# Agent attention with a routed feed-forward on one core: the folded units' matrix in one pass, its low part on spare rows

## The chip, the cores and the metric

The kernel runs on one core of a Trainium2 chip. The metric is the device time of one execution in microseconds (us). Three timed runs of the kernel before gave 667.96, 669.16 and 669.85 us; their median is 669.16 us. A fourth execution was profiled: it took 664.34 us, of which 662.6 us lie between the first and the last instruction, and all rows below are of this one.

## The reference

Four batches of 11,456 tokens with 128 channels go through an attention over 49 agents, and then through a layer of eight experts of which each token takes one.

```
def sm(a, b):
    s = scale * (a @ b.transpose(0, 2, 1))
    s = s - s.max(-1, keepdims=True)
    e = np.exp(s)
    return e / (e.sum(-1, keepdims=True) + 1e-09)
a2k = sm(agents, k)
agent_v = a2k @ v
q2a = sm(q, agents)
x = q2a @ agent_v
...
expert_idx = np.argmax(logits, axis=1)          # logits: cosine of x and each expert's row, over tau
for e in range(E):
    mask = expert_idx == e
    h = np.maximum(x[mask] @ w1[e], 0.0)
    out[mask] = gate_w[mask, None] * (h @ w2[e])
```

Here E is 8, w1 is 128 by 1024 and w2 is 1024 by 128 for each expert.

## The kernel before, in words

**A token is 49 exponentials.** Its x is a mix of 49 agent rows. The kernel never forms x: it keeps the token's 49 exponentials e, multiplies the agent rows into the expert's first matrix once a batch (one row g of 49 numbers for each of the 1024 hidden units), and computes a hidden unit as relu(g . e). The division by the sum of e, and the gate, come at the end as one factor per token.

**Three kinds of units.** All e are positive, so a unit whose g has mostly one sign keeps its sign over nearly all tokens. `pick_expert(b, g)` takes one expert for the whole batch, gives each unit a key for how much its sign is in doubt, and ranks the units by it. The `FM` = 256 units in most doubt are computed in full as a layer (`gh`, `gl`, the high and low float16 parts of their g, and `w2p`, their rows of w2). The others are taken as always on or always off: those that are on are summed into one 49 by 128 matrix, `lin`, so that their share of the output is e times `lin`. The next `FV` = 288 units in rank are checked for every token, by a product with `vm` (their g, times their sign, less a safety margin): the first `NEAR` = 32 with a minimum for each token (`vmin`), the other 256 with a sum of negative parts for each pair of tokens (`vsum`). For the units beyond, one bound on the token (`far`) does. Tokens that fail, or whose expert is another one, are done again at the end in full (`mark_strays`, `fix`, `stray`): 128 places a batch in `fix`, one group in `stray_first`, and what is then left in a loop at the end of the program (L1740), of one pass for each 128 places.

**Operands.** `q_unit` makes the exponentials of a unit of 8 columns of 128 tokens: 128 partitions (tokens) by 8 columns by 128 places, of which places 0 to 48 hold the high float16 part, 64 to 112 the low part, and the 30 others zero. A transposing DMA on the queue of SP (SyncE) turns each column, so that `tt` has the 128 places on partitions. There are 48 such units, 12 a batch.

**Tiles.** The feed-forward goes over 92 tiles (23 a batch) of four columns, 512 tokens (the last of a batch has two columns of 96). `ffn_mm1` (L1237, L1238) does a half of 128 layer units by two matmuls of 512 columns; ScalarE takes the relu into a high part (L1246), VectorE the low part (L1247). `ffn_mm2` adds into the tile's `yp`, at f = 0, the folded part: for each column two matmuls of 128 columns, one with the high and one with the low part of `lin` (L1261). Then each of the two halves gives three matmuls a column (L1273 to L1275; L1270 for tiles from 16 on of the first three batches). VectorE multiplies by the gate into `ot` (L1289), and ScalarE's queue stores it.

```
1258:            for c in range(n):
1259:                tc_ = tts[b, u][:, (w * TJ + c) * p : (w * TJ + c + 1) * p]
1260:                for h in range(2):
1261:                    pe.matmul(out=yp[:p, c, :], lhsT=tc_, rhs=bt.lin[:, h], start=(c == 0 and h == 0), stop=False, skip_group_check=True)
```

**The check.** `proved` does a unit's check in five jobs: 8 matmuls of 32 columns and VectorE's minimum (L1092, L1095), and four pairs of matmuls of 256 columns with ScalarE's sum (L1089, L1098).

**Order.** Beside the feed-forward of a batch the kernel loads the keys, values and queries of the next one by a plan of due times, makes its scores and its exponentials, and near the batch's end runs `pick_expert` for the next. SP's queue stands in an order written out; on the other engines a scheduler that runs a model of the program sets the order, so that an edit in one place moves instructions elsewhere too.

Of the kernel before, what the change touches and what calls it, by code (L numbers as in the profile page):

```python
# [29 lines left out]
def kernel(ctx: ExitStack, tc: tile.TileContext, q, k, v, agents, emb, tau, w1, w2, out):  # L30
# [8 lines left out]
    NEAR = 32  # L39
    FV = 2 * P + NEAR  # L40
    FM = NM * P
    FW = 4 * P
# [13 lines left out]
    LO = 64  # L56
# [243 lines left out]
    tri = cst.tile([P, P], F16, name="tri")  # L300
    uid = cst.tile([P, NF], I32, name="uid")
# [22 lines left out]
    def setup():  # L324
# [4 lines left out]
        with tc.issue_after(turned[0].ins):  # L329
# [7 lines left out]
            dve.tensor_tensor(out=fold, in0=ident[:, :A], in1=ident[:, LO : LO + A], op=ALU.add)  # L337
            pool.iota(tok[:, :, :J], pattern=[[N, B], [1, J]], base=0, channel_multiplier=J,
# [236 lines left out]
    def av_chain(b, g):  # L575
# [45 lines left out]
        dve.tensor_copy(r_hi[:, E : E + 1], ones[:, :1])  # L621
# [48 lines left out]
    def pick_expert(b, g):  # L670
# [173 lines left out]
        gmx = sm.tile([P, 2], F32, name="gmx", tag="gmx")  # L844
        yield 2 * g
        act.copy(gh, placed(0, FM))
        yield g
        dve.tensor_copy(gl, placed(1, FM))
        bt.gh, bt.gl = gh, gl
        dve.tensor_reduce(out=gmx[:, :1], in_=ga, axis=AX.XY, op=ALU.max, apply_absolute_value=True)  # L850
# [4 lines left out]
        dve.tensor_scalar(mask, rank, FM + FV - 0.5, BIG, ALU.is_lt, ALU.mult)  # L855
# [3 lines left out]
        dve.tensor_reduce(out=gmx[:, 1:], in_=mask, axis=AX.X, op=ALU.min)  # L859
        yield 1  # L860
        dve.tensor_scalar(gmx[:, 1:], gmx[:, 1:], -1.0, None, ALU.mult)
        dve.tensor_scalar(mask, rank, FM - 0.5, None, ALU.is_ge)
        yield 1
        dve.scalar_tensor_tensor(out=mask, in0=sgn, scalar=0.0, in1=mask, op0=ALU.is_gt, op1=ALU.mult)
        yield 1
        for h in (1, 0):
            pool.tensor_tensor(out=gts[:, :, h, :A], in0=ga, in1=mask.unsqueeze(2).broadcast_to([P, NF, A]), op=ALU.mult)
# [7 lines left out]
        dve.scalar_tensor_tensor(out=lin[:, 1], in0=t_[:, :D], scalar=ls_, in1=lin[:, 0], op0=ALU.mult, op1=ALU.subtract)  # L875
        bt.lin = lin
# [3 lines left out]
        for f in range(0, NM, 2):  # L880
# [7 lines left out]
            yield g  # L888
        bt.w2p = w2p
# [20 lines left out]
        dve.tensor_scalar(vm, t_, thr, None, ALU.subtract)  # L910
# [20 lines left out]
    def q_unit(b, u, g):  # L931
# [29 lines left out]
        pool.tensor_tensor(out=e2[:p, :n, LO : LO + A], in0=e, in1=hi, op=ALU.subtract)  # L961
        tt = wk.tile([P, UJ * P], F16, name="tt", tag="tt", bufs=TB)
# [145 lines left out]
    def mark_strays(b):  # L1108
# [45 lines left out]
        yield 1  # L1154
        dve.tensor_copy(cnt, t_[:, :1])
# [4 lines left out]
        dve.tensor_scalar(last, cnt, P - KEEP + 0.5, BIG, ALU.is_gt, ALU.mult)  # L1160
# [89 lines left out]
    def ffn_mm2(b, t, f):  # L1250
# [523 lines left out]
```

## Time and profile before

| what | value |
|---|---|
| median of three timed runs | 669.16 us |
| the profiled execution | 664.34 us |
| its span, first to last instruction | 662.6 us |
| TensorE matmuls (PE), busy | 631.3 us, 95% |
| TensorE weight loads (PEld), busy | 540.1 us, 82% |
| VectorE (DVE), busy | 513.8 us, 78% |
| ScalarE (ACT), busy | 458.7 us, 69% |
| GpSimd (POOL), busy | 345.7 us, 52% |
| mean granted TensorE clock | 0.996 of full |

Busy time is the time in which at least one instruction of the engine is under way. Matmuls overlap each other, so that the time from one start to the next, not the duration of one, is what a matmul costs in a row of them. The first 84.5 us hold the keys and values of batch 0; the first tile of the feed-forward starts at 84.6 us, and tiles 23, 46 and 69, the first of the other batches, at 241.0, 393.4 and 545.2 us.

### The profile page before, as it was taken

The numbers are of one execution on the slowest core, as the hardware profiler recorded it, in microseconds if no ns is written. First come the engines' busy times: TensorE is split into PE (matmuls) and PEld (weight loads), VectorE is DVE, ScalarE is ACT, GpSimd is POOL, SyncE is SP. The second block draws the span as 40 slices with busy tenths as digits, with TensorE's granted clock in tenths as the row PEclk, the third lists the DMA queues.
The fourth block names the chain that finished last, engine by engine and source line by source line (L and its number), as shares of the span: only waits on it lengthen the run. The fifth ranks groups of instructions, "written<-read, shape, count | busy, mean of one in ns | idle before, by whom it ended". The sixth has DMA issues, their size and how long they took to land. (4 is left out here: it accounts for less than half of the span.)

```text
span 662.6 us, 23329 instructions
## 1 busy us (share of the span) xinstructions
PE 631.3 (95%) x9299; PEld 540.1 (82%) x9299; DVE 513.8 (78%) x1487; ACT 458.7 (69%) x1147; POOL 345.7 (52%) x592
## 2 busy tenths in 40 slices
PE   8988999999999999999999889999999999999996
PEld 6887878888887877888888787888888897787886
DVE  5777798687776898876786889986576979896793
ACT  3537846877678956886777965876479855987642
POOL 6003284386135566783623684684655755877310
PEclk9989999999999999999999999999999999999999
DMA  8997397599686249999859455998568434314422
GB/s 341 286 348 212 57 342 194 125 226 286 180 265 188 64 118 217 285 295 230 216 182 245 120 114 147 264 282 217 130 196 216 102 65 138 62 34 137 142 101 76
DMA packets 157049, 123.33 MB, mean 186 GB/s; under 512 B 76753, under 2 KB 133155, under 8 KB 156939
## 3 DMA queue, kind: packets, MB, share of 16 engines
q1 hardware_dynamic: 143499, 97.97, 58.8%
q10 hardware_dynamic: 13120, 23.47, 10.2%
q8 instruction: 74, 1.21, 0.8%
q0 software_dynamic: 320, 0.38, 0.2%
q14 instruction: 36, 0.29, 0.1%
HBM read 80.26 MB, written 23.79 MB: 157 GB/s over the span
## 5 line engine op out<-in xcount | busy, mean ns | idle before, releaser
L1098 ACT ACTIVATE vp<-vp 128x512 f32<-128x512 f32 x180 | 106.4, 591 | 17.3 <-PE vp L1089 15.0
L1246 ACT ACTIVATE hh<-hp 128x512 f16<-128x512 f32 (+1 forms) x142 | 83.1, 592 | 47.9 <-PE hp L1238 32.6
L1247 DVE SCALAR_TENSOR_TENSOR hh<-hp,hh 128x512 f16<-128x512 f32 (+1 forms) x142 | 95.5, 676 | 26.3 <-ACT hh L1246 25.6
L1274 PE MATMUL yp<-w2p,hh 128*128 128x128 f16 x564 | 107.3, 219 | 0.0
L1273 PE MATMUL yp<-w2p,hh 128*128 128x128 f16 x564 | 107.0, 219 | 0.0
L1275 PE MATMUL yp<-w2p,hh 128*128 128x128 f16 x564 | 105.6, 219 | 0.3 <-DVE hh L1247 0.3
L449 PE MATMUL sp<-aT_all,fT 128*64 128x49 f32 x2496 | 95.9, 224 | 1.9 <-DVE vm L910 1.0
L449 PEld LDWEIGHTS sp<-aT_all,fT 128*64 128x64 f32 x2496 | 83.8, 137 | 15.9 <-issue 4.6
L441 ACT COPY fT<-fTp 128x512 f32<-128x512 f32 (+1 forms) x115 | 62.9, 572 | 31.1 <-PE fTp L436 20.7
L961 POOL TENSOR_TENSOR e<-qe,e 128x392 f16<-128x392 f32 (+1 forms) x48 | 43.0, 897 | 64.2 <-ACT e L958 53.0
L1237 PE MATMUL hp<-tt,gh 128*128 128x512 f16 (+1 forms) x184 | 68.7, 373 | 4.0 <-DVE hh L1247 1.8
L1089 PE MATMUL vp<-vm,tt 128*128 128x256 f16 x360 | 69.7, 273 | 0.7 <-DVE vmin L1095 0.6
L1036 POOL TENSOR_TENSOR nrm<-qq,half 128x16 f32<-128x16 f32 (+2 forms) x28 | 69.0, 2464 | 0.2
L1289 DVE TENSOR_TENSOR ot<-yp,gs 128x512 f32<-128x512 f32 (+1 forms) x92 | 61.5, 670 | 9.2 <-PE yp L1275 5.3
L1238 PE MATMUL hp<-tt,gl 128*128 128x512 f16 (+1 forms) x184 | 68.6, 373 | 0.0
L1261 PE MATMUL yp<-lin,tt 128*128 128x128 f16 x720 | 62.4, 219 | 2.2 <-DVE ot L1289 2.1
L1273 PEld LDWEIGHTS <-hh 128*128 128x128 f16 x564 | 55.4, 98 | 6.4 <-issue 0.7
L1275 PEld LDWEIGHTS <-hh 128*128 128x128 f16 x564 | 55.4, 98 | 6.1 <-DVE hh L1247 0.4
L1274 PEld LDWEIGHTS <-hh 128*128 128x128 f16 x564 | 55.5, 98 | 4.8 <-issue 0.5
L1261 PEld LDWEIGHTS <-tt 128*128 128x128 f16 x720 | 48.4, 99 | 9.9 <-issue 4.4
L997 POOL TENSOR_TENSOR rt<-rt 128x384 f32<-128x384 f32 (+1 forms) x48 | 40.7, 848 | 29.0 <-DVE rt L994 14.1
L436 PE MATMUL fTp<-ident,qt 128*128 128x128 f32 x360 | 54.2, 281 | 0.9 <-ACT vp L1098 0.4
(372 smaller groups left out, 1636.7 us busy)
## 6 DMA issues: line engine op xcount, KB each, us to landing
kt<-in_k_dram SPq DMA_DIRECT2D x44, 512.0 KB, 6.5
vt<-in_v_dram SPq DMA_DIRECT2D x44, 512.0 KB, 6.4
qt<-in_q_dram SPq DMA_DIRECT2D x44, 512.0 KB, 5.4
out_dram<-ot ACTq DMA_DIRECT2D x88, 256.0 KB, 3.5
w1s<-in_moe_w_dram SPq DMA_DIRECT2D x9, 512.0 KB, 4.2
w2s<-in_moe_w_dram SPq DMA_DIRECT2D x9, 512.0 KB, 5.3
tt<-e SPq DMA_TRANSPOSE x48, 4.6
kt<-in_k_dram SPq DMA_DIRECT2D x4, 96.0 KB, 8.5
```

The costliest lines, as they stand in the source:

```text
L449: pe.matmul(out=s[h : h + w, c * A : (c + 1) * A], lhsT=xT[:, c * p + h : c * p + h + w], rhs=aT_all[:, b, :], start=True, stop=True, skip ...
L1036: pool.tensor_tensor(out=nrm, in0=quad, in1=half[:, :n], op=ALU.pow)
L1089: pe.matmul(out=z[:p, i * FP : (i + 1) * FP], lhsT=tt[:, c * p : (c + 1) * p], rhs=bt.vm[:, NEAR:], start=True, stop=True)
L1098: act.activation(z[:p], z[:p], AF.Relu, scale=-1.0, accum_out=bt.vsum[:p, at : at + 1])
L1237: pe.matmul(out=hp[:, :m], lhsT=bt.gh[:, fs], rhs=tt, start=True, stop=False)
L1238: pe.matmul(out=hp[:, :m], lhsT=bt.gl[:, fs], rhs=tt, start=False, stop=True)
L1246: h_last[:] = [act.activation(hh[:, :m], hp[:, :m], AF.Relu)]
L1247: dve.scalar_tensor_tensor(out=hl[:, :m], in0=hp[:, :m], scalar=0.0, in1=hh[:, :m], op0=ALU.max, op1=ALU.subtract)
L1261: pe.matmul(out=yp[:p, c, :], lhsT=tc_, rhs=bt.lin[:, h], start=(c == 0 and h == 0), stop=False, skip_group_check=True)
L1273: pe.matmul(out=y, lhsT=hh[:, cs], rhs=wh, start=False, stop=False, skip_group_check=True)
L1274: pe.matmul(out=y, lhsT=hh[:, cs], rhs=wl, start=False, stop=False, skip_group_check=True)
L1275: y_last[:] = [pe.matmul(out=y, lhsT=hl[:, cs], rhs=wh, start=False, stop=last, skip_group_check=True)]
```

## The change

The low part of `lin` no longer has a pass of its own. It has 49 rows, one for each agent. The rows of agents 19 to 48 (30 of them) go to the 30 spare partitions of `tt`: `q_unit` copies the exponentials of these agents there, and the single matrix `lin[:, 0]` holds the high part on the 98 partitions of before and the low part on the 30. The rows of agents 0 to 18 go through the layer: 19 of the 256 places get a g of one at one agent, so that the layer gives this agent's e, and their rows of `w2p` are the low part. So 237 units are left in the layer (`FN`), and `iotah` numbers the places around the 19. The check takes 320 units, 64 of them with a minimum for each token. Its margin is now a share of each entry rather than of the largest, which takes a ScalarE step (Abs) ahead of `vm` and no longer VectorE's largest entry over all. The bound `far` loses less (0.005 for 0.1), and a partition's strays are kept while they fit in 128 places in all.

```diff
-    NEAR = 32
+    NEAR = 64
     FV = 2 * P + NEAR
     FM = NM * P
+    LO = 64
+    XA = A - 2 * (LO - A)
+    FN = FM - XA
...
+            dve.tensor_reduce(out=mrow[:, :1], in_=fold, axis=AX.X, op=ALU.add)
+            dve.tensor_scalar(mrow[:, 1:], mrow[:, :1], -1.0, 1.0, ALU.mult, ALU.add)
+            pmem(iotah, -1.0)
+            pool.tensor_copy(iotah[:, :P], iotaf[:, :P])
+            pool.tensor_copy(iotah[:, P + XA :], iotaf[:, P:FN])
...
         act.copy(gh, placed(0, FM))
+        act.copy(gh[:, P : P + XA], fold[:, :XA])
...
-        dve.tensor_reduce(out=gmx[:, :1], in_=ga, axis=AX.XY, op=ALU.max, apply_absolute_value=True)
...
+        for h in (1, 0):
+            m_ = LO - A
+            a_ = XA + h * m_
+            pool.tensor_tensor(out=gts[:, :, h, A:], in0=ga[:, :, a_ : a_ + m_], in1=mask.unsqueeze(2).broadcast_to([P, NF, m_]), op=ALU.mult)
...
+        dve.tensor_scalar(lin[:, 0], lin[:, 0], mrow[:, :1], None, ALU.mult)
+        dve.scalar_tensor_tensor(out=lin[:, 0], in0=lin[:, 1], scalar=mrow[:, 1:], in1=lin[:, 0], op0=ALU.mult, op1=ALU.add)
...
+        act.copy(w2p[:XA, 1, 0], lin[:XA, 1])
...
-        dve.tensor_scalar(thr, top[:, :1], 1.05 * 2.0 ** -11, None, ALU.mult)
-        dve.tensor_scalar(bt.far, top[:, 1:], A + 0.1, None, ALU.add)
+        dve.tensor_scalar(bt.far, top, A + 0.005, None, ALU.add)
...
-        dve.tensor_scalar(vm, t_, thr, None, ALU.subtract)
+        aw = gts.rearrange("p c h a -> p (c h a)")[:, :FV]
+        act.activation(aw, t_, AF.Abs, scale=2.1 * 2.0 ** -11)
+        dve.scalar_tensor_tensor(out=vm, in0=t_, scalar=2.0 ** -22, in1=aw, op0=ALU.subtract, op1=ALU.subtract)
...
+        pool.tensor_copy(e2[:p, :n].rearrange("p c (h k) -> p c h k", h=2)[:, :, :, A:], e[:, :, XA:].rearrange("p c (h k) -> p c h k", h=2))
...
+        own = sm.tile([P, 1], F32, name="had3", tag="had3", bufs=1)
+        dve.tensor_tensor(out=own, in0=t_[:, :1], in1=cnt, op=ALU.add)
...
-        dve.tensor_scalar(last, cnt, P - KEEP + 0.5, BIG, ALU.is_gt, ALU.mult)
+        dve.tensor_scalar(last, own, P + 0.5, BIG, ALU.is_gt, ALU.mult)
...
-                for h in range(2):
-                    pe.matmul(out=yp[:p, c, :], lhsT=tc_, rhs=bt.lin[:, h], start=(c == 0 and h == 0), stop=False, skip_group_check=True)
+                pe.matmul(out=yp[:p, c, :], lhsT=tc_, rhs=bt.lin[:, 0], start=(c == 0), stop=False, skip_group_check=True)
```

Line numbers move: L1261 is L1279 now, L961 is L977, and L875 is L888.

On TensorE, where the first tiles of batch 0 are begun (`hp` are the layer's sums of a tile, `linp` the matrix `lin` before it is split, `w2pp` the layer's rows of w2), there stood before:

```order
L871 MATMUL linp_1659<-w2s_859,gts_152 128x128 x8
L1237 MATMUL hp_1592<-tt_942,gh_1041 128x512
L1237 MATMUL hp_1629<-tt_942,gh_1041 128x512
L1261 MATMUL yp_1706<-lin_1045,tt_942 128x128
L1261 MATMUL yp_1919<-lin_1045,tt_942 128x128
L885 MATMUL w2pp_1671<-w1s_858,sel_154 128x256
```

and now stands:

```order
L884 MATMUL linp_1672<-w2s_866,gts_152 128x128 x8
L1256 MATMUL hp_1603<-tt_950,gh_1050 128x512
L1256 MATMUL hp_1640<-tt_950,gh_1050 128x512
L900 MATMUL w2pp_1686<-w1s_865,sel_154 128x256
L445 MATMUL fTp_1656<-ident_82,qt_1533 128x128 x4
L458 MATMUL sp_1743<-aT_all_116,fT_1655 64x49 x8
L1256 MATMUL hp_1764<-tt_950,gh_1050 128x512
```

The passes with `lin` have moved behind the 16 matmuls of `w2pp`, some scores and the next tile's `hp`, and they are half as many: 720 in the whole program before, 360 now.

On VectorE, at the same place (`lin` is the pair of high and low part, `sel` the places of the units to be checked), there stood before:

```order
L878 SCALAR_TENSOR_TENSOR w1s_858<-w2s_859,hsc_1505,w1s_858 128x8x128
L994 TENSOR_TENSOR rt_1477<-rtp_1459,qe_1140 128x392
L875 SCALAR_TENSOR_TENSOR lin_1045<-linp_1659,hsc_1505,lin_1045 128x128
L1247 SCALAR_TENSOR_TENSOR hh_1595<-hp_1592,hh_1595 128x512
L905 TENSOR_SCALAR sel_154<-iotaf_155,rank_1307,sgn_1051 128x288 x5
```

and now stands:

```order
L893 SCALAR_TENSOR_TENSOR w1s_865<-w2s_866,hsc_1516,w1s_865 128x8x128
L888 SCALAR_TENSOR_TENSOR lin_1054<-linp_1672,hsc_1516,lin_1054 128x128
L1266 SCALAR_TENSOR_TENSOR hh_1606<-hp_1603,hh_1606 128x512
L889 TENSOR_SCALAR lin_1054<-lin_1054,mrow_159 128x128
L919 TENSOR_SCALAR sel_154<-iotaf_155,rank_1318,sgn_1060 128x320 x7
L890 SCALAR_TENSOR_TENSOR lin_1054<-lin_1054,mrow_159 128x128
```

The matrix is whole two steps later, and the second of them stands behind the eight selections.

On GpSimd, where the first four units' exponentials are made (`qe` are the exponentials, `e16` the operand of the transposing DMA), there stood before:

```order
L961 TENSOR_TENSOR e16_1_151<-qe_963,e16_1_151 128x8x49
L818 TENSOR_TENSOR gt16_153<-gts_152,gt16_153 128x8x49 x2
L961 TENSOR_TENSOR e16_0_150<-qe_1140,e16_0_150 128x8x49
L867 TENSOR_TENSOR gts_152<-gts_152,mask_1532 128x8x49
L961 TENSOR_TENSOR e16_1_151<-qe_1212,e16_1_151 128x8x49
```

and now stands:

```order
L978 CAST e16_1_151<-qe_971 128x16x15
L977 TENSOR_TENSOR e16_1_151<-qe_971,e16_1_151 128x8x49
L827 TENSOR_TENSOR gt16_153<-gts_152,gt16_153 128x8x49 x2
L978 CAST e16_0_150<-qe_1149 128x16x15
L977 TENSOR_TENSOR e16_0_150<-qe_1149,e16_0_150 128x8x49
L978 CAST e16_1_151<-qe_1222 128x16x15
L878 TENSOR_TENSOR gts_152<-gts_152,mask_1543 128x8x15 x2
L880 TENSOR_TENSOR gts_152<-gts_152,mask_1543 128x8x49
L977 TENSOR_TENSOR e16_1_151<-qe_1222,e16_1_151 128x8x49
```

The scheduler has put the new copy ahead of the subtraction that makes the low part, not behind it as the code has it.

## Rows read from the trace of the kernel before

**Rows 1.** The page's first part: busy time, share of the span, instructions of each engine.

```profile
span 662.6 us, 23329 instructions
PE 631.3 (95%) x9299; PEld 540.1 (82%) x9299; DVE 513.8 (78%) x1487; ACT 458.7 (69%) x1147; POOL 345.7 (52%) x592
```

**Rows 2.** Windows: length, busy us (instructions) of PE, PEld, DVE, ACT, POOL; clock, DMA.

```profile
84.50:120.00 35.50, 34.00 (x491) 28.80 (x487) 29.69 (x79) 20.00 (x52) 19.18 (x35) 1.00 0.79 234
120.00:205.00 85.00, 84.63 (x1330) 72.75 (x1331) 63.63 (x157) 63.73 (x159) 42.70 (x65) 1.00 0.85 223
205.00:265.00 60.00, 55.60 (x776) 47.06 (x775) 51.98 (x159) 45.08 (x110) 37.51 (x68) 1.00 0.57 143
265.00:365.00 100.00, 100.00 (x1534) 86.69 (x1533) 74.86 (x203) 76.53 (x191) 53.04 (x79) 1.00 0.95 242
365.00:440.00 75.00, 69.86 (x1039) 59.17 (x1038) 67.20 (x204) 56.39 (x140) 52.86 (x90) 1.00 0.72 173
440.00:540.00 100.00, 98.51 (x1341) 84.63 (x1339) 70.44 (x190) 73.45 (x189) 59.31 (x91) 1.00 0.70 173
540.00:605.00 65.00, 60.94 (x947) 52.04 (x945) 57.53 (x206) 48.05 (x146) 46.05 (x73) 1.00 0.34 82
605.00:657.00 52.00, 50.28 (x630) 42.53 (x627) 40.31 (x118) 26.96 (x68) 12.65 (x28) 1.00 0.37 122
```

**Rows 3.** Windows of L1261 alone: length, PE busy (matmuls), PEld busy, clock, DMA.

```profile
120.00:205.00 85.00, 9.07 (x104) 7.00 (x104) 1.00 0.85 223
265.00:365.00 100.00, 11.65 (x128) 8.83 (x128) 1.00 0.95 242
440.00:540.00 100.00, 10.60 (x120) 8.05 (x120) 1.00 0.70 173
605.00:657.00 52.00, 8.50 (x108) 6.95 (x108) 1.00 0.37 122
```

**Rows 4.** Timeline of PE: start, length, instructions in a row of one kind.

```profile
647.35 0.61 PE L1261 MATMUL yp<-lin,tt 128*128 128x128 f16 x8
...
613.76 0.35 PE L1092 MATMUL vp<-vm,tt 128*128 128x32 f16 x8
...
80.77 0.19 PE L976 MATMUL rtp<-r_hi,tt 128*128 128x58 f16 x1
...
81.14 0.19 PE L976 MATMUL rtp<-r_hi,tt 128*128 128x58 f16 x1
```

**Rows 5.** Groups by line and form: busy us, mean ns of one, idle before.

```profile
L1247 DVE SCALAR_TENSOR_TENSOR hh<-hp,hh 128x512 f16<-128x512 f32 x140 | 94.8, 681 | 26.1 <-ACT hh L1246 25.6
L1095 DVE TENSOR_REDUCE vmin<-vp 128x8 f32<-128x256 f32 x44 | 18.3, 416 | 7.0 <-PE vp L1092 6.9
L850 DVE TENSOR_REDUCE gmx<-gts 128x1 f32<-128x392 f32 x4 | 2.2, 555 | 1.2 <-ACT gts L736 1.2
L961 POOL TENSOR_TENSOR e<-qe,e 128x392 f16<-128x392 f32 x44 | 41.1, 934 | 64.2 <-ACT e L958 53.0 <-issue 10.4 <-POOL rtg L125 0.6
L196 POOL CAST ident<-ident 128x128 f16<-128x128 f32 x1 | 0.3, 327 | 2.1 <-DVE ident L194 2.1
L958 ACT CAST e<-qe 128x392 f16<-128x392 f32 x44 | 23.4, 532 | 0.4
```

**Rows 6.** Windows of VectorE's L1095 alone, in the three stretches where batches change.

```profile
205.00:265.00 60.00, 1.88 (x5) 1.00 0.57 143
365.00:440.00 75.00, 2.27 (x6) 1.00 0.72 173
540.00:605.00 65.00, 4.30 (x11) 1.00 0.34 82
```

**Rows 7.** Windows of all engines, columns of rows 2: the last tiles.

```profile
621.00:652.00 31.00, 31.00 (x434) 26.07 (x432) 28.85 (x87) 14.27 (x31) 4.37 (x11) 1.00 0.35 123
```

**Rows 8.** Timeline of POOL: the last gather and the last write of strays.

```profile
639.59 1.52 POOL L1322 DMA_INDIRECT xq<-in_q_dram,ix  x1 [0.79 <-DVE ix L1400]
657.63 1.03 POOL L1387 DMA_INDIRECT out_dram<-so,ix  x1 [16.52 <-DVE so L1384]
```

More of the change, by code (lines that the diff above doesn't have):

```diff
@@ L55 @@
     SCALE = 1.0 / math.sqrt(C)
-    LO = 64
     FP = 2 * P
@@ L300 @@
     tri = cst.tile([P, P], F16, name="tri")
+    iotah = cst.tile([P, FM], F16, name="iotah")
+    mrow = cst.tile([P, 2], F32, name="mrow")
     uid = cst.tile([P, NF], I32, name="uid")
@@ L620, in av_chain @@
         r_lo = sm.tile([P, RW], F16, name="r_lo", tag="r_lo")
-        dve.tensor_copy(r_hi[:, E : E + 1], ones[:, :1])
+        dve.tensor_copy(r_hi[:, E : E + 1], mrow[:, :1])
         pmem(r_lo[:, E : E + 1], 0.0)
@@ L829, in pick_expert @@
         for c in range(NF):
-            dve.tensor_scalar(sel[:, c, :FM], iotaf[:, :FM], rank[:, c : c + 1], None, ALU.is_equal)
+            dve.tensor_scalar(sel[:, c, :FM], iotah, rank[:, c : c + 1], None, ALU.is_equal)
             if c % 4 == 3:
@@ L842, in placed @@
             return t_
-        gmx = sm.tile([P, 2], F32, name="gmx", tag="gmx")
+        gmx = sm.tile([P, 1], F32, name="gmx", tag="gmx")
         yield 2 * g
         act.copy(gh, placed(0, FM))
+        act.copy(gh[:, P : P + XA], fold[:, :XA])
         yield g
@@ L854, in pick_expert @@
         mask = col("mask")
-        dve.tensor_scalar(mask, rank, FM + FV - 0.5, BIG, ALU.is_lt, ALU.mult)
+        dve.tensor_scalar(mask, rank, FN + FV - 0.5, BIG, ALU.is_lt, ALU.mult)
         yield 1
@@ L858, in pick_expert @@
         yield 1
-        dve.tensor_reduce(out=gmx[:, 1:], in_=mask, axis=AX.X, op=ALU.min)
+        dve.tensor_reduce(out=gmx, in_=mask, axis=AX.X, op=ALU.min)
         yield 1
-        dve.tensor_scalar(gmx[:, 1:], gmx[:, 1:], -1.0, None, ALU.mult)
-        dve.tensor_scalar(mask, rank, FM - 0.5, None, ALU.is_ge)
+        dve.tensor_scalar(gmx, gmx, -1.0, None, ALU.mult)
+        dve.tensor_scalar(mask, rank, FN - 0.5, None, ALU.is_ge)
         yield 1
@@ L894, in pick_expert @@
         bt.iall = iall
-        dve.tensor_scalar(rank, rank, -float(FM), None, ALU.add)
+        dve.tensor_scalar(rank, rank, -float(FN), None, ALU.add)
         yield 1
         yield 2 * g
-        top = yield from allmax(gmx, 2, "gmxr", psx, 1 + 3 * g, 2, lambda: in_place(y_last if b > 0 else []))
-        thr = sm.tile([P, 1], F32, name="thr", tag="thr")
+        top = yield from allmax(gmx, 1, "gmxr", psx, 1 + 3 * g, 2, lambda: in_place(y_last if b > 0 else []))
         bt.far = sm.tile([P, 1], F32, name="far", tag="far")
-        dve.tensor_scalar(thr, top[:, :1], 1.05 * 2.0 ** -11, None, ALU.mult)
-        dve.tensor_scalar(bt.far, top[:, 1:], A + 0.1, None, ALU.add)
+        dve.tensor_scalar(bt.far, top, A + 0.005, None, ALU.add)
         yield 1
```

## The prediction

> **What bounds the kernel now.** I read the page's busy shares first [rows 1]. TensorE's matmuls are busy 95% of the span, VectorE 78%, ScalarE 69%, GpSimd 52%. An average over stages decides nothing, so I cut the time from the first tile (84.5 us) to the last store into stretches [rows 2]. Two kinds are to be seen. In three stretches (120 to 205, 265 to 365, 440 to 540 us) TensorE is busy 84.63 of 85, 100.00 of 100 and 98.51 of 100 us, while VectorE stands at 70 to 75%: there TensorE alone sets the pace. In the four around the changes of batch (84.5 to 120, 205 to 265, 365 to 440, 540 to 605) TensorE has 34.00 + 55.60 + 69.86 + 60.94 = 220.4 of 235.5 us, 94%, and VectorE 29.69 + 51.98 + 67.20 + 57.53 = 206.4, 88%: neither is full, and each waits for the other in turn. The last tiles (605 to 657) come close to the first kind. The granted clock is 1.00 in every stretch, so no time goes to the slower level there.
>
> **What the removed passes are worth.** L1261 has 720 matmuls, and 360 go. How many lie in each kind of stretch is in [rows 3]: 104 + 128 + 120 = 352 in the full ones, 108 in the last, so 720 - 352 - 108 = 260 in the mixed ones. A row of eight takes 0.61 us [rows 4]; with 0.22 for the last one's own length, the other seven starts are (0.61 - 0.22) / 7 = 55.7 ns apart. That is the price of one, not the length of 219 ns that overlaps its neighbours. All 360 make 20.0 us of TensorE.
>
> **What TensorE gets in their place.** The 360 check matmuls of L1092 go from 32 to 64 columns. Eight of 32 columns take 0.35 us [rows 4], a pitch of (0.35 - 0.18) / 7 = 24 ns. The trace has none of 64. At 58 columns fifteen starts lie between 80.77 and 81.14 us, 26.4 ns apart; a line from there to 55.7 ns at 128 columns gives 28.9 at 64. So a matmul costs 2.4 to 4.9 ns more, and all of them 0.9 to 1.8 us; I take 1.4, as 58 columns are the nearest row. The Trainium skill's page "TensorE: Matmul & The Clock Gate" (the section on 56 and 53.3 ns) says why doubling is nearly free: starts never come closer than about 25 ns however small the matmul is, and above that cost columns over 2.4 GHz plus 2.5 ns. The trace agrees at 32 columns (24 ns). By the page's formula, an estimate, 64 columns take 29.2 ns and the term would be 1.9 us. The `placed` product gains 32 columns in 32 matmuls: 32 x 32 x 55.7 / 128 = 0.45 us. Together TensorE loses 20.0 and gains 1.85: 18.2 us less.
>
> **What VectorE gets.** The minimum of L1095 goes from 256 to 512 columns. It takes 416 ns at 256, and VectorE's passes over 512 columns of PSUM take 681 (L1247) [rows 5], so I add 0.265 us to each, 44 times: 11.7 us. Of the 48 checks 5 + 6 + 11 = 22 lie in the three later mixed stretches [rows 6], and I count two more in the first. The largest entry (L850, 4 x 0.555 us) goes; two steps on `lin` come, 128 columns each and so under 0.68, and a longer selection: small, and near even.
>
> **The sum, stretch by stretch.** In the full stretches 176 x 55.7 ns = 9.8 us go, and half of TensorE's additions (0.9) come: 8.9 less. VectorE, ScalarE and GpSimd have 20 us and more in each hundred to spare, so all of it should show.
>
> In the last tiles 54 x 55.7 ns = 3.0 us go. But from 621 to 652 us VectorE is busy 28.85 of 31 us beside a full TensorE [rows 7]; after 2.15 us less there VectorE is full. I take 2.0, between 0 and 3.0.
>
> In the mixed stretches TensorE loses 130 x 55.7 ns = 7.2 less 0.9 = 6.3 us, and VectorE gains 24 x 0.265 = 6.4. If TensorE decided everywhere it would be 6.3 less, if VectorE did, 6.4 more. TensorE's idle share (6%) is half of VectorE's (12%), so I let it decide two thirds: 2/3 x 6.3 - 1/3 x 6.4 = 2.1 less.
>
> The start of batch 0 gains a longer chain to a whole `lin`: two half passes over its matrix on GpSimd, two steps on VectorE behind the eight selections. By the order TensorE has the `w2pp` matmuls, scores and the next `hp` ahead of the first pass with `lin`, which cover it; without that cover it is two steps of at most 0.68 each. I charge 0.5 once. The extra copies of the setup and the ScalarE steps (Abs, 19 rows of `w2p`) fall where their engines are idle, and cost nothing.
>
> GpSimd's copy of the 30 rows is 240 elements a partition. The cast of 128 takes 327 ns, the two-input pass over 392 takes 934 [rows 5], so 0.33 to 0.93 us; I take 0.5, near the cast. 48 of them are 24 us on an engine at 52%. What hides it is the wait before L961: GpSimd stands idle 64.2 us there, 53.0 of them for ScalarE's cast L958 (532 ns), and the order has the new copy ahead of the subtraction, in that wait. I charge nothing. Without that cover each unit would be turned 0.5 us later, then SP's queue behind the transposing DMA, then the routing product.
>
> Sum: 8.9 + 2.0 + 2.1 - 0.5 = 12.5 us less than the profiled execution's 664.34, 651.8. That execution was 0.7% below the median of the timed runs; I take the ratio, 651.8 / 664.34 = 0.981, to the median: 669.16 x 0.981 = 656.6 us.
>
> **The rivals.** About 0.3%, 2 us, is what a measurement of this kernel can tell from no change.
>
> *All of it shows.* TensorE decides in the mixed and last stretches too: 8.9 + 3.0 + 6.3 = 18.2 less, 651 us. For it speaks that TensorE is the fuller engine in every stretch; against it VectorE's 88 to 93%.
>
> *VectorE takes over where batches change and in the last tiles:* 8.9 + 0 - 6.4 - 0.5 = 2.0 less, 667 us; with half of that taking over 662.
>
> *TensorE is not full.* The removed passes could fill time in which TensorE waits for the relu's two parts anyway; then nothing shows, 669 us. For it speaks that the weight loads are busy only 86.69 of 100 us from 265 to 365 [rows 2]; against it that a matmul of 512 columns needs one load as a matmul of 128 does, so that this share stays low in a full TensorE, and that VectorE has a quarter of that stretch free. The Trainium skill's page "Perfetto Trace Analysis" (Identifying the Most-Contended Engine) speaks for it: matmul busy time is a bad measure there, and the weight loads' share the better one.
>
> *The turned exponentials come late.* If one in four of the 48 copies lay on the path, 12 x 0.5 = 6 us come back, 663; with all of them 24, and the kernel is slower by 12.
>
> *One pass of the loop for strays (slower).* Stricter and looser bounds change how many tokens `fix` has to hold. Evaluating the rules on the reference's inputs gives 128 flagged tokens in batch 0 where 124 were, for 128 places. One more, and a partition's tokens go to the loop at the program's end, which the trace does not enter now. A pass costs at least what stands between the last gather and the end of the last write, 657.63 + 1.03 - 639.59 = 19.1 us [rows 8]: 676 us. The nearest unflagged token misses the bounds by a few ten-thousandths, far above float32 rounding, so this is unlikely.
>
> That the passes stay is excluded: the order has 360.
>
> **How the numbers follow.** Forecast (653 to 661 us) 0.50; all of it 0.17; VectorE takes over 0.15; not full 0.08; late turning 0.06; a stray pass 0.04. Faster by over 0.3% are the first two and 0.13 of the others: 0.80. Within 0.3% are most of "not full" and the ends of two more: 0.12. Slower 0.08. The range goes from 648 (the best case of 651 with 0.5% below it) to 667 us, where VectorE's case ends; outside lie "not full", the loop and half of the late turning.
>
> **What the profile after would show.** L1261 with 360 matmuls, 55.7 ns apart. L1092 with 64 columns, eight in 0.37 to 0.39 us. L1095 near 0.68 us. The three full stretches shorter by about 3 us each for the same tiles, with TensorE still over 98%; VectorE about 2 points busier. GpSimd's copy near 0.5 us, in front of L961, whose wait for ScalarE shrinks by as much. As many gathers of strays as now, or the loop was entered. I am wrong if the full stretches keep their length, if TensorE's idle time in the mixed ones grows by more than 6 us, or if TensorE waits for `tt`.

## The result, and the profile after

The changed kernel takes 674.11 us (median of four runs, 673.34 to 674.84) where the kernel before took 669.5 beside it: a ratio of 1.0081, 95% interval 1.0061 to 1.0102. The change made it 0.8% slower; the forecast was 1.9% faster. (Ratios, here and below, are of runs taken side by side, and can differ by some 0.2% from the quotient of two medians.)

The first part of the page after (busy time of each engine, its share, instructions):

```profile
span 671.6 us, 22694 instructions
PE 622.9 (93%) x8939; PEld 525.8 (78%) x8939; DVE 532.3 (79%) x1493; ACT 459.9 (68%) x1159; POOL 364.3 (54%) x651
```

Against [rows 1] the 360 matmuls are gone, but TensorE's matmuls are busy only 8.4 us less, and the time without one grew from 662.6 - 631.3 = 31.3 to 48.7 us. So 17.4 us without a matmul came in. The windows after, columns and bounds of [rows 2]:

```profile
84.50:120.00 35.50, 33.04 (x487) 27.62 (x485) 30.93 (x82) 20.42 (x55) 21.33 (x40) 1.00 0.79 251
120.00:205.00 85.00, 84.72 (x1297) 71.42 (x1295) 66.45 (x156) 65.44 (x161) 44.28 (x68) 1.00 0.89 221
205.00:265.00 60.00, 52.74 (x693) 44.25 (x692) 52.86 (x153) 43.24 (x106) 37.01 (x72) 0.97 0.56 126
265.00:365.00 100.00, 96.83 (x1488) 83.44 (x1485) 77.85 (x205) 72.68 (x186) 56.51 (x89) 0.98 0.90 239
365.00:440.00 75.00, 66.65 (x913) 54.66 (x909) 67.36 (x200) 57.16 (x141) 47.22 (x84) 1.00 0.65 160
440.00:540.00 100.00, 97.13 (x1305) 82.02 (x1306) 70.64 (x186) 73.59 (x190) 65.85 (x105) 1.00 0.73 192
540.00:605.00 65.00, 58.12 (x907) 49.27 (x906) 61.21 (x208) 47.52 (x144) 45.34 (x76) 1.00 0.33 68
605.00:657.00 52.00, 48.45 (x577) 39.36 (x577) 43.94 (x126) 29.50 (x79) 22.26 (x45) 0.97 0.40 131
```

Two of the three full stretches are less full (96.83 and 97.13 of 100 us, where 100.00 and 98.51 stood), and the granted clock, 1.00 everywhere before, is below it in three stretches. What TensorE waits for (in total, times, longest):

```profile
PE yp L1279 <- DVE ot L1307: 6.6, 5, 3.7
PE hp L1256 <- DVE hh L1266: 2.5, 2, 2.2
PE mB L225 <- DVE mTx L221: 2.4, 3, 1.4
PE rtp L993 <- DMA tt<-e: 2.2, 2, 1.4
PE vp L1106 <- DVE vmin L1112: 2.0, 2, 1.3
```

The longest three, in the timeline after (start, length, engine, instruction, in brackets the wait before it):

```profile
211.60 0.34 POOL L1010 TENSOR_TENSOR rt<-qe 96x98 f32<-96x98 f32 x1
211.83 5.62 DVE L425 TENSOR_TENSOR m_run<-s_u,m_run 128x392 f32<-128x392 f32 x1 [2.68 <-ACT s_u L531]
211.91 2.03 POOL L759 TENSOR_TENSOR w2s<-w2s,hsc 128x512 f32<-128x512 f32 x2
213.90 0.90 POOL L977 TENSOR_TENSOR e<-qe,e 128x392 f16<-128x392 f32 x1
214.76 2.26 POOL L760 TENSOR_TENSOR w1s<-w2s,w1s 128x512 f16<-128x512 f32 x2
217.37 1.27 DVE L1307 TENSOR_TENSOR ot<-yp,gs 128x512 f32<-128x512 f32 x2
218.10 0.48 PE L1279 MATMUL yp<-lin,tt 128*128 128x128 f16 x3 [3.67 <-DVE ot L1307]
...
288.65 1.28 DVE L1307 TENSOR_TENSOR ot<-yp,gs 128x512 f32<-128x512 f32 x2
289.38 0.38 PE L1279 MATMUL yp<-lin,tt 128*128 128x128 f16 x4 [2.08 <-DVE ot L1307]
...
634.39 1.13 POOL L1405 DMA_INDIRECT out_dram<-so,ix  x1 [1.39 <-DVE had L1165]
636.12 0.60 ACT L1265 ACTIVATE hh<-hp 128x512 f16<-128x512 f32 x1 [0.30 <-PE had L1170]
638.42 0.34 ACTq L1313 DMA_DIRECT2D out_dram<-ot  x1
638.86 0.60 ACT L1265 ACTIVATE hh<-hp 128x512 f16<-128x512 f32 x1 [2.15 <-DMA out_dram<-so,ix]
640.24 0.38 PE L1256 MATMUL hp<-tt,gh 128*128 128x512 f16 x1 [2.15 <-DVE hh L1266]
```

At 211.83 VectorE begins a running maximum that reads two tiles in SBUF. Its median is 0.555 us; here it lasts 5.62, to 0.4 us behind the end of GpSimd's row of six steps (217.02), and the `ot` that TensorE needs stands behind it. At 287 us `ot` is late again. At 636 us a store on ScalarE's queue waits for the write of strays (L1405), and the relus stand behind the store. Behind each of these three waits the clock falls to the lower of its levels, 1.2 GHz, as the windows of these places show:

```profile
218.00:221.40 3.40, 3.30 (x16) 2.87 (x16) 3.40 (x7) 2.03 (x5) 0.00 (x0) 0.50 1.09 251
289.70:293.10 3.40, 3.40 (x23) 2.77 (x21) 2.59 (x6) 1.72 (x6) 2.40 (x4) 0.50 1.02 299
641.30:644.70 3.40, 2.99 (x28) 2.91 (x29) 2.78 (x11) 0.60 (x1) 0.86 (x2) 0.50 0.43 159
```

Three times 3.4 us at half speed is up to 5.1 us. Between the first tile and the last the kernel before had no time at this level.

Where the time went, tile by tile: the same first-layer matmul (L1237, L1256 now) is looked up in each trace at the tile nearest to each bound of [rows 2], and the table has by how much each stretch became longer (+) or shorter. e1 and e2 are experiments told below. In the forecast's column the mixed stretches have their 2.1 us less and the 0.5 charged to the chain. The table says where time went, less surely how much: the profiled execution of the kernel before, 664.34 us, is one of its fast ones, that of the changed kernel, 673.34, is near its median, so that the +10.0 here stands against 4.6 us between the medians. The time ahead of the first tile (+0.9 after) and behind the last (-1.9) is not in it.

| stretch (starts before) | kind | forecast | after | e1: all work, old order | e2: single pass, old order |
|---|---|---|---|---|---|
| 84.6 to 119.4 | mixed | | +0.1 | +3.2 | -1.1 |
| 119.4 to 204.8 | full | | -1.8 | -1.4 | -2.0 |
| 204.8 to 266.6 | mixed | | +3.5 | +1.3 | -1.3 |
| 266.6 to 363.2 | full | | +1.0 | -1.4 | -1.3 |
| 363.2 to 439.8 | mixed | | +0.1 | +4.0 | +1.0 |
| 439.8 to 540.3 | full | | +2.5 | -1.0 | -3.5 |
| 540.3 to 605.0 | mixed | | -0.2 | +1.9 | +0.3 |
| 605.0 to 646.0 | last | -2.0 | +4.8 | -2.5 | -2.5 |
| all full | | -8.9 | +1.7 | -3.8 | -6.8 |
| all mixed | | -1.6 | +3.5 | +10.4 | -1.1 |
| first to last tile | | -12.5 | +10.0 | +4.1 | -10.4 |

### The profile page after: what moved, and what is told of

Read it like the earlier page. It is cut to its first block, busy times and chain, and to the rows that moved or that the text cites. A ratio compares the mean times of both kernels' runs of the same rounds, so it can differ in the third digit from the quotient of the medians.

```text
span 671.6 us, 22694 instructions
## 1 busy us (share of the span) xinstructions
PE 622.9 (93%) x8939; PEld 525.8 (78%) x8939; DVE 532.3 (79%) x1493; ACT 459.9 (68%) x1159; POOL 364.3 (54%) x651
## 3 DMA queue, kind: packets, MB, share of 16 engines
q10 hardware_dynamic: 13120, 23.47, 10.2%
## 5 line engine op out<-in xcount | busy, mean ns | idle before, releaser
L1256 PE MATMUL hp<-tt,gh 128*128 128x512 f16 (+1 forms) x184 | 69.3, 377 | 7.5 <-DVE hh L1266 2.5
L978 POOL CAST e<-qe 128x240 f16<-128x240 f32 (+1 forms) x48 | 17.9, 374 | 79.1 <-ACT qe L969 71.0
L445 PE MATMUL fTp<-ident,qt 128*128 128x128 f32 x360 | 56.1, 285 | 3.0 <-ACT vp L1115 1.3
L977 POOL TENSOR_TENSOR e<-qe,e 128x392 f16<-128x392 f32 (+1 forms) x48 | 41.6, 866 | 14.2 <-ACT e L974 14.0
L557 PE MATMUL avp<-vt,kd 128*64 128x129 f32 x720 | 48.5, 278 | 0.3 <-issue 0.3
```

The lines of the kernel that those rows point to most:

```text
L1256: pe.matmul(out=hp[:, :m], lhsT=bt.gh[:, fs], rhs=tt, start=True, stop=False)
```

## The experiments

Three theories stood at the start. **O**: the order that the scheduler made anew costs the gain. **W**: the change's own work on VectorE and GpSimd does. **N**: TensorE was never full. Ratios are to the kernel before in runs on the same chip, with 95% intervals; that kernel's single runs there lay between 663 and 674 us, so a microsecond of difference says nothing.

To hold an order, an edge of issue order was set from each instruction of an engine to the next; `PINNED` holds, for the four engines, the places of the instructions in the order wanted (SP's order is the same in all; the code is shortened, `PINNED` stands for the packed lists):

```diff
+    for eng, steps in PINNED.items():
+        row = [by[eng][at] for at in steps]
+        for a_, b_ in zip(row, row[1:]):
+            tc.add_manual_dep(b_, a_.name, mybir.DependencyInfo(mybir.DependencyClass.NoSync, mybir.DependencyReason.DATA), reason="pinned")
```

The edges themselves cost nothing that shows: e16 and e17 below hold the orders of e8 and e6 but for one move, and take 1.0047 and 1.0033 where those, without edges, took 1.006 and 1.0017.

**e1, all work in the old order.** The edit is the one above, with the order of before.

> The changed kernel, all of it, but with TensorE, VectorE, ScalarE and GpSimd held to the order in which the kernel before had these instructions; the 80 or so new ones stand beside the instruction that they belong to. Theory O (the new order is at fault: it puts VectorE's and ScalarE's work where TensorE comes to wait for it): 650 to 660 us, near the forecast of 656.6. Theory W (the change's own work on VectorE and GpSimd takes up what TensorE was given): 670 to 676, as the changed kernel. Theory N (TensorE was never full, so that removed matmuls give nothing): 669 or more.

672.28 us, 1.0033 (0.999 to 1.0076). By the ratios the order is worth some 3 us of the loss, with intervals that overlap (the changed kernel's is 1.0061 to 1.0102), and not all of it: **O** alone falls.

**e2, the single pass alone in the old order.**

```diff
-                for h in range(2):
+                for h in range(1):
```

> The kernel before in its own order, with the 360 matmuls of the low part left out and nothing else changed (so the low part of the folded matrix is missing from the output). Theories O and W: 649 to 654, that is the 18 to 20 us of TensorE less. Theory N: 667 to 670.

657.48 us, 0.982 (0.9754 to 0.9886): some 12 us, not 20, and between what the theories had said. In the trace the removed matmuls are all there to see: from the first to the last tile the starts of L1261, each counted from the start of the matmul ahead of it, add up to 29.8 us where they were 49.2, 19.4 less. But the starts of all other matmuls, counted in the same way, are 9.0 us further apart in all. Nearly half of the gain comes back in this way, although nothing was added and no order changed. The windows of e2 over the tiles of the three full stretches (columns of [rows 2]):

```profile
122.01:205.41 83.40, 82.66 (x1283) 70.13 (x1280) 63.36 (x157) 63.78 (x160) 42.48 (x65) 1.00 0.88 227
265.95:361.20 95.25, 93.83 (x1433) 80.29 (x1431) 72.04 (x195) 72.96 (x183) 52.17 (x74) 1.00 0.99 251
438.88:535.80 96.92, 96.09 (x1285) 81.74 (x1283) 70.14 (x190) 73.32 (x189) 59.51 (x91) 1.00 0.74 178
```

Matmuls are busy 272.58 of 275.57 us, still 99%, after 9.8 us of them were taken out and 6.8 us of time went. Of what came back there, only 1.1 us is idle time of TensorE (1.9 before, 3.0 here); the rest lies in longer steps between the starts of matmuls that overlap. A busy share near 100% did not say that every microsecond taken out would show: matmuls of 0.22 us that start 0.056 us apart cover small waits between them. **N** is right in part.

**e3 and e4, one piece of added work less, in the changed kernel's own order.** e3 leaves out GpSimd's copy, e4 halves the minimum:

```diff
-        pool.tensor_copy(e2[:p, :n].rearrange("p c (h k) -> p c h k", h=2)[:, :, :, A:], e[:, :, XA:].rearrange("p c (h k) -> p c h k", h=2))
...
-            dve.tensor_reduce(out=bt.vmin[:p, at : at + n], in_=z[:p, : n * NEAR].rearrange("p (c f) -> p c f", f=NEAR), axis=AX.X, op=ALU.min)
+            dve.tensor_reduce(out=bt.vmin[:p, at : at + n], in_=z[:p, : n * NEAR].rearrange("p (c f) -> p c f", f=NEAR)[:, :, : NEAR // 2], axis=AX.X, op=ALU.min)
```

> The changed kernel in its own order, without GpSimd's 48 copies of the 30 rows (so the low part of 30 agents is missing from the output). Theory O: 670 to 675, as with the copies. Theory W in the form that GpSimd's longer work holds up VectorE where both read the same memory: 655 to 665.

> The changed kernel in its own order, where VectorE's minimum reads 32 of the 64 columns (so half of these checks have no effect). It takes some 0.25 us off each of 48 steps. Theory O: 670 to 674. Theory W in the form that VectorE's longer minimum decides: 660 to 666.

675.8 us, 1.0118 (1.0052 to 1.0183), and 673.77, 1.0067 (1.0031 to 1.0103). Neither gives back anything that shows (the intervals leave room for some 3 us), and the three long waits stand in both traces where they stood (3.6 and 3.7 us at 218, 2.3 and 1.8 at 290, 2.2 and 2.4 at 640). With either piece of work gone they are still there; they belong to the order, which is the same in all three.

**e5, the three waits mended.** The first of the moves, on VectorE:

```diff
-L425 TENSOR_TENSOR m_run<-s_u,m_run 128x392
 L1307 TENSOR_TENSOR ot<-yp,gs 128x512 x2
+L425 TENSOR_TENSOR m_run<-s_u,m_run 128x392
```

> The changed kernel with all its work, held to its own order except at the three longest waits of TensorE. At 212 us VectorE's two products into ot go ahead of the running maximum that stood 5.6 us behind GpSimd's row of six steps; at 287 us the gate's reciprocal, the ScalarE step behind it and one product into ot go ahead of their neighbours; at 637 us two of ScalarE's relus go ahead of the stores that wait for the write of strays. Theory O (waits that the order makes, and the clock's lower level behind them, took up the gain): the waits of 3.7, 2.1 and 2.2 us shrink, the lower level at these places may go too, and the time falls by 5 to 13 us, to 661 to 669. Theory W (VectorE and GpSimd have too much to do there, so that a wait taken away at one place comes back at the next): within 2 us of the changed kernel.

671.9 us, 1.0043 (1.0003 to 1.0082), some 2.5 us better than the changed kernel, with intervals that overlap. The maximum, two steps later, still ends only after GpSimd's row; TensorE no longer waits at 214, but it does at 219.7. The timeline of e5:

```profile
211.87 1.29 DVE L1307 TENSOR_TENSOR ot<-yp,gs 128x512 f32<-128x512 f32 x2 [2.87 <-ACT gs L1084]
213.07 4.24 DVE L425 TENSOR_TENSOR m_run<-s_u,m_run 128x392 f32<-128x392 f32 x1
219.73 0.20 PE L993 MATMUL rtp<-r_hi,tt 128*96 128x58 f16 x1 [1.39 <-DVE qe L967]
```

Of 4.0 us won by tile 20, 1.6 are gone by tile 23; the second place gives 0.5 and the third 0.2. The lower clock is gone from the first two places and still there at the third.

**e6, e7 and e8, other orders.** e6 is e2 without the edges, so in an order of the scheduler's. e7 and e8 are the changed kernel and the kernel before with one priority moved:

```diff
-                    with tc.high_priority(200):
+                    with tc.high_priority(190):
                         ffn_mm1(b, t, f)
```

> The kernel before without the 360 matmuls of the low part (which is missing from the output), this time in the order that the scheduler makes for it. The same work in the old order gained 1.8%. Theory O: a new order alone can cost some of this, so the gain is anywhere between 0 and 2.5% and differs from 1.8% by 0.5 or more. Theory W: 1.6 to 2.0% again, since no work was added.

> The changed kernel with one number of the scheduler's moved (the priority of the layer's first matmuls, 200 to 190), which changes no work and gives another order of it on all four engines. Theory O: the time moves by more than 3 us to either side, and the waits at 214, 287 and 638 us stand elsewhere or are gone. Theory W: 671 to 677 again.

> The kernel before with the same number moved in the same way (no work changed, another order). It shows how much an order is worth where no work changes. Theory O: it moves by more than 3 us, rather up, as the order of before was a good one: 672 to 680. Theory W: within 2 us of the kernel before.

e6: 669.89 us, 1.0017 (0.9977 to 1.0056). The same instructions that gain 1.8% in the old order gain nothing in the new one. e7: 678.7, 1.0126 (1.0047 to 1.0205). e8: 672.22, 1.006 (1.0018 to 1.0102). Three new orders of three kernels, and each is slower than it would be in the old one or than it was. Two of them are clear of the noise, e6 against e2 and e8 against the kernel before; e7's interval overlaps the changed kernel's. That a new order alone can cost time, as **O** has it, is shown.

**e9, e10, e11 and e13: what the added work costs in the old order.** e9 and e10 take away what e3 and e4 did; e11 takes off the chain to the folded matrix

```diff
...
-            m_ = LO - A
-            a_ = XA + h * m_
-            pool.tensor_tensor(out=gts[:, :, h, A:], in0=ga[:, :, a_ : a_ + m_], in1=mask.unsqueeze(2).broadcast_to([P, NF, m_]), op=ALU.mult)
...
-        dve.tensor_scalar(lin[:, 0], lin[:, 0], mrow[:, :1], None, ALU.mult)
-        dve.scalar_tensor_tensor(out=lin[:, 0], in0=lin[:, 1], scalar=mrow[:, 1:], in1=lin[:, 0], op0=ALU.mult, op1=ALU.add)
```

and e13 all three.

> The changed kernel in the old order, without GpSimd's 48 copies (the low part of 30 agents is missing from the output). In the old order the changed kernel took 1.003 of the time before, the single pass alone 0.982: 14 us are the added work's. If the copies make VectorE wait behind a longer row of GpSimd steps (3.7 us for one step of the gate at 447 us, then 2.1 us of TensorE), 3 to 5 us of them come back here; if GpSimd's wait hides them, as the forecast had it, none.

> The changed kernel in the old order, with VectorE's minimum over 32 of the 64 columns (half of these checks have no effect). Of 48 steps 24 lie in the stretches where batches change. If VectorE decides there, 3 to 6 us come back; if TensorE does, less than 2.

> The changed kernel in the old order, without the two VectorE steps that set the low part into the folded matrix and without GpSimd's two products for its 30 rows (so the matrix has no low part on them). TensorE waited 3.0 us for this matrix at 93.5 us, with the lower clock behind it, 1.2 us for GpSimd's products at 240 us, and 2.1 us at 403 us for a relu's low part that stood behind these steps. If this chain costs what its waits show, 6 to 10 us come back; by the forecast's charge, 0.5.

> The changed kernel in the old order without all three: GpSimd's copies, half of VectorE's minimum, and the chain's two VectorE steps and GpSimd products (outputs as said for each). If the three parts add up (2 + 0 + 6): 663 to 665, 0.993 of the time before. If each stood behind the others: 658 to 661, near the single pass alone at 0.982.

e9: 669.47 us, 1.0007 (0.9982 to 1.0032). e10: 671.06, 1.0032 (1.0008 to 1.0057). e11: 664.54, 0.9942 (0.9913 to 0.9971). e13: 660.96, 0.9901 (0.9869 to 0.9933). Against e1's 1.0033 the copies are worth 0.3%, within the intervals; the minimum nothing, to within some 3 us; the chain 0.9%, 6 us. The three together are worth 1.3%, near the sum of 1.2%; the intervals are too wide to say more. From e13 to e2 0.8% is left, of which TensorE's own columns are 1.85 us (0.3%); the intervals touch, and no more is made of it.

**e12, e14 and e18: all work, the old order, the chain mended.** e12 moves the steps that some of the waits of e1 point to. Among the longest are these four:

```profile
PE yp L1279 <- DVE lin L890: 3.0, 1, 3.0
PE mB L225 <- DVE mTx L221: 2.9, 3, 1.6
PE hp L1256 <- DVE hh L1266: 2.1, 1, 2.1
...
PE linp L884 <- POOL gts L880: 1.9, 2, 1.2
```

One of the five moves, in batch 0 on VectorE:

```diff
+L888 SCALAR_TENSOR_TENSOR lin<-linp,hsc,lin 128x128
+L889 TENSOR_SCALAR lin<-lin,mrow 128x128
+L890 SCALAR_TENSOR_TENSOR lin<-lin,mrow 128x128
 L893 SCALAR_TENSOR_TENSOR w1s<-w2s,hsc,w1s 128x8x128
...
-L888 SCALAR_TENSOR_TENSOR lin<-linp,hsc,lin 128x128
...
```

e14 makes the matrix in one step of VectorE (`lm` is one on the 30 rows and zero on the others, in batch 0 times the scale; a second step, off the path, makes the 19 rows for `w2p`). e18 makes the products in fewer steps of GpSimd:

```diff
-        act.activation(lin[:, 0], t_[:, :D], AF.Copy, scale=ls_)
...
+        act.activation(lin[:, 1], t_[:, :D], AF.Copy, scale=lm)
+        dve.scalar_tensor_tensor(out=lin[:, 0], in0=t_[:, :D], scalar=ls_, in1=lin[:, 1], op0=ALU.mult, op1=ALU.subtract)
...
+        pool.tensor_tensor(out=ga, in0=ga, in1=mask.unsqueeze(2).broadcast_to([P, NF, A]), op=ALU.mult)
+        act.copy(gts[:, :, 1, :A], ga)
...
+            pool.tensor_copy(gts[:, :, h, A:], ga[:, :, a_ : a_ + m_])
```

> The changed kernel with all its work in the old order, but with five moves: in batch 0 the three steps that make the folded matrix go ahead of the split of w1; at batch 2 the relu's low part goes ahead of them; at 247 us the largest entry goes ahead of two selections; GpSimd's two products of a batch stand together twice. Theory O: the waits of 3.0, 2.1, 1.6 and 1.2 us shrink and with them the lower clock at two places: 660 to 666, the changed kernel below the kernel before. Theory W: within 2 us of the old order without them, 669 to 673.

> The changed kernel with all its work in the old order and the five moves, with the folded matrix made in one VectorE step where it took three: ScalarE takes the high part times a mask that is one on the 30 rows and zero on the others, and VectorE's product less this is the high part on the one and the low part on the other rows. If the chain of VectorE steps is what e11 found dear: 663 to 667, 0.994 to 0.998 of the time before, below both kernels. If it is GpSimd's two products, which stay: 669 to 671.

> The version of the run with the one-step chain, all work done, in the old order. GpSimd now makes one masked product of 49 columns a batch where it made two of 49 and two of 15; ScalarE copies it to the second half while GpSimd copies the 30 rows, so that the matrix product can start 0.8 to 1.0 us sooner in each of four batches, about as soon as in the kernel before. If GpSimd's products are the dear half of the chain: 662 to 666, 0.991 to 0.997 of the time before and below both kernels. If neither half is, but VectorE's two steps beside the path, 667 to 669 as without it.

e12: 670.16 us, 1.0026 (0.9999 to 1.0052). e14: 667.81, 0.9995 (0.9971 to 1.0018). e18: 667.54, 0.9989 (0.9959 to 1.0018). No step alone is clear of the noise, and the three together, 0.4% from e1 to e18, are not either. e18, 0.9% below the changed kernel, is the best with all the work done and cannot be told from the kernel before. So no version of this change beat it. Of the chain's 6 us some 3 seem to come back by making it shorter; the rest left only when the work did.

**e16 and e17: one late step of the new orders.** In e6 and e8 the same VectorE step stands behind the same row of GpSimd's. The timeline of e6:

```profile
367.16 0.34 POOL L993 TENSOR_TENSOR rt<-qe 96x98 f32<-96x98 f32 x1
367.22 5.73 DVE L502 SCALAR_TENSOR_TENSOR ks<-kt,hsc,ks 128x512 f16<-128x512 f32 x2 [1.25 <-ACT ks L494]
367.46 2.03 POOL L750 TENSOR_TENSOR w2s<-w2s,hsc 128x512 f32<-128x512 f32 x2
369.46 2.27 POOL L751 TENSOR_TENSOR w1s<-w2s,w1s 128x512 f16<-128x512 f32 x2
376.60 0.27 PE L1092 MATMUL vp<-vm,tt 128*128 128x32 f16 x4 [3.49 <-DVE fT L439]
```

```diff
-L502 SCALAR_TENSOR_TENSOR ks<-kt,hsc,ks 128x512 x2
-L822 TENSOR_SCALAR_CACHE_REDUCE sel<-sel,key 128x8x128 x2
 L948 TENSOR_REDUCE qmx<-sp 128x8x49
 L439 COPY fT<-fTp 128x512
+L502 SCALAR_TENSOR_TENSOR ks<-kt,hsc,ks 128x512 x2
+L822 TENSOR_SCALAR_CACHE_REDUCE sel<-sel,key 128x8x128 x2
```

> The kernel before in the other order that took 1.006, with one move: at 372 us the two VectorE steps that make the low part of the keys, of which the first stood 4.9 us behind GpSimd's row of steps, go behind the maximum and the copy that TensorE waits for. If that one step is what this order loses: TensorE's wait of 3.3 us goes, and the time falls by 3 to 5 us to the kernel before's, 668 to 670. If it is a loss all over the order: within 1 us of 672.

> The single pass in the scheduler's own order (1.002), with the same one move at 367 us, where the same step stood 5.1 us and TensorE 3.5. If that step is what this order loses there: 3 to 5 us less, 0.994 to 0.997 of the time before. If it is a loss all over: within 1 us of 670.

e16: 672.19 us, 1.0047 (1.0022 to 1.0073). e17: 669.83, 1.0033 (1.0002 to 1.0064). Neither moved. The wait of 3.3 us is gone from e16, but VectorE stood 4.1 us for the scores instead, its three long steps (L822) now stood ahead of the step that TensorE needs next (L951), and TensorE waited 2.4 us for that. The timeline of e16:

```profile
373.83 0.57 DVE L948 TENSOR_REDUCE qmx<-sp 128x8 f32<-128x392 f32 x1 [4.10 <-PE sp L449]
374.31 0.68 DVE L439 COPY fT<-fTp 128x512 f32<-128x512 f32 x1
378.13 0.38 PE L1237 MATMUL hp<-tt,gh 128*128 128x512 f16 x1 [0.87 <-ACT fT L441]
381.11 0.19 PE L976 MATMUL rtp<-r_hi,tt 128*96 128x58 f16 x1 [2.39 <-DVE qe L951]
```

There a move hands the wait to the next step.

**e19, the best code in the scheduler's order.**

> The same code in the order that the scheduler makes for it. Theory O: a new order loses the 3 to 12 us that it lost with the single pass (e6), the kernel before (e8) and the changed kernel (e7): 670 to 678. Theory W: the shorter chain helps in any order: 664 to 669.

675.62 us, 1.0102 (1.007 to 1.0134), 1.1% above the same code in the old order.

## Why the prediction was wrong

**The step that failed** is "The sum, stretch by stretch", in three of its terms. First, "so all of it should show": the full stretches were to give 8.9 us and became 1.7 longer, and even where nothing else changes 9.8 us of matmuls taken from them are worth 6.8 (e2). Second, a term that the sum has at nothing, without a reason: it took the order as it stood, though the order is made anew. New orders cost 12 us with the same instructions (e6 against e2), 8 (e19 against e18), 4 with no change of work (e8); for the change as it is the ratios say about 3 (1.0081 against e1's 1.0033), with intervals that overlap. Third, the price of the added work. The single pass alone in the old order gives 1.8%, nearly the whole forecast; with the added work this order stands at 1.0033. So the added work costs some 14 us there, where the sum had charged about 4 (0.9 in the full stretches, 2.7 in the mixed ones, 0.5 for the chain). Between the scheduler's own orders the same work costs some 4 us (1.0081 against e6's 1.0017): its price hangs on the order too, and the terms do not simply add up.

Two of the forecast's signs of being wrong came: the full stretches did not get shorter, and TensorE's idle time in the mixed windows grew by 9.9 us, from 15.1.

**Point by point.** *The removed passes* were priced rightly: 360 went, four in a row take 0.38 us, and they make 19.4 us in e2. *TensorE's additions* too: the starts of L1109 are 29 ns apart where 28.9 was said, and eight take 0.40 us. *VectorE's minimum* has the length said (0.68), but of the 2 to 6 us charged to it nothing shows: e4 and e10 give nothing back, to within some 3 us. The rows after:

```profile
L1112 DVE TENSOR_REDUCE vmin<-vp 128x8 f32<-128x512 f32 x44 | 29.9, 680 | 2.5 <-PE vp L1109 2.4
L978 POOL CAST e<-qe 128x240 f16<-128x240 f32 x44 | 17.0, 387 | 79.0 <-ACT qe L969 70.8 <-issue 7.9 <-DMA tt<-e 0.2
L977 POOL TENSOR_TENSOR e<-qe,e 128x392 f16<-128x392 f32 x44 | 40.1, 911 | 14.1 <-ACT e L974 14.0
```

*GpSimd's copy* takes 0.39 us for 0.5 and lies in the wait for ScalarE, as said: what L977 waits fell from 64.2 us [rows 5] to 14.1. That it costs nothing is neither shown nor refuted (e9 is 0.3% better, within the intervals). *The chain to `lin`* was charged 0.5 us once, for batch 0, and is the most mis-sized term: the chain stands in each of the four batches, and e11 gives 6 us back. Its added steps (L878, L889 and L890) are 6.5 us long together in e1, so they cost about their own length. Some of it comes by way of the clock: in e1 TensorE waits 3.0 us for `lin` at 93.5 us, and 2.1 us at 403 for a relu's low part that stands behind the chain's steps, and after both the clock is at its lower level, as these windows of e1 show. e11's trace has it at neither place.

```profile
96.60:100.00 3.40, 3.40 (x19) 2.49 (x18) 2.34 (x7) 0.00 (x0) 2.31 (x2) 0.50 1.13 291
407.20:414.00 6.80, 6.68 (x63) 5.18 (x64) 5.69 (x25) 2.81 (x8) 1.93 (x5) 0.50 0.75 222
```

The cover that the forecast saw was there in the new order (0.2 us of wait for L890 after), which is one thing the new order did better. *The mixed stretches* were to give 6.3 or cost 6.4; in the old order the single pass gives 1.1 of 7.2, and with all work they are 10.4 longer. So TensorE decides far less than two thirds there. But VectorE's busy time does not decide either: with half of the minimum gone they are still 10.5 longer (e10), while without the chain they are 4.3 longer (e11; one trace each). What shows is the chain of steps in which each engine waits for the other, and the sum had no term for it beyond batch 0. *The last tiles* give the 2.5 us in the old order (forecast 2.0), and lose 4.8 in the new one. The longest wait there is that of the relus behind the stores and the write of strays, but with two relus moved ahead of the stores (e5) 4.6 of it stay, so the cause of this loss is open.

**The rivals.** "VectorE takes over" is not borne out: VectorE's longer minimum, on which it stood, gives nothing back (e10). "TensorE is not full" holds for a third of the full stretches' gain; the Trainium skill's page "Perfetto Trace Analysis" (Identifying the Most-Contended Engine) had spoken for it. A turned operand that is late is a small part: TensorE waits 2.2 us for `tt`, 1.3 before. The loop for strays was not entered: five gathers, as before. The rival that was missing is a worse order with the same work.

**What stays open.** Where exactly a new order loses its 4 to 12 us is not settled. The long waits that can be pointed to were moved in e5, e12, e16 and e17 and gave back 2.5, 0.5, 1 and -1 us by the ratios, none of it clear of the noise; in e5 and e16 the wait turned up again a little later. The clock has a part in it. Between the first tile and the last it is at its lower level for no time in the traces of the kernel before and of e2, 3.4 us in e8 and e11, 6.8 in e18, and 10.2 in the changed kernel, e1, e6 and e19, which at half speed is up to 5.1 us.

## What to carry to other kernels

Where a scheduler sets the order, an edit is two changes: its own, and a new order. Hold the old order and measure the edit in it before the edit is judged; and set the old order's luck beside it by an edit that changes no work. Where two engines are near 90%, taking work from one of them gives little (1.1 of 7.2 us here), and steps added to a chain that both wait for can cost their whole length in every batch, although each engine has idle time.

## What the runs showed of the hardware

A VectorE step that reads two tiles in SBUF can wait not for one GpSimd step but for a whole row of them: 5.62 us for a step of 0.555, behind six steps that followed each other without a gap, and the same at 4.24 us (e5), 5.06 and 4.88 (L502 in e6 and e8, where the second of the pair took 0.74). The Trainium skill's page "SBUF — State Buffer" (Who interferes with whom) has the rule: such a VectorE instruction and a GpSimd instruction that reads SBUF exclude each other, and the second to issue waits for the whole of the first. The trace agrees, and adds that in these rows VectorE was not let in between two GpSimd steps. It is not always so. In the kernel before the same running maximum (L416 there) began 0.6 us into a GpSimd step of such a row (L798), and the timeline has:

```profile
211.19 0.84 DVE L416 TENSOR_TENSOR m_run<-s_u,m_run 128x392 f32<-128x392 f32 x1
211.56 2.37 POOL L750 TENSOR_TENSOR w2s<-w2s,hsc 128x512 f32<-128x512 f32 x2
```

It took 0.84 us, and this time the next GpSimd step was the one that waited: the first of L750's two took 1.37 us, the second 1.04. What decides which goes first is open, and whether a gap in the row would let VectorE in was not tried.

The granted clock was at its lower level for 3.4 us in the first 84 us of the kernel before but for 13.7 in e2's, with the same work there, so the profiled executions' spans differ by some microseconds for no reason in the edit. The window of e2:

```profile
47.50:61.50 14.00, 13.73 (x119) 12.76 (x117) 7.78 (x27) 5.07 (x11) 1.71 (x2) 0.51 0.67 224
```
